# Six turns of K and q moved in the slot plan of an attention and SwiGLU kernel, two clearings moved forward

## The chip, the cores and the metric

The kernel runs on one core of a Trainium2 chip. The metric is the time of one execution on the device, in microseconds (us), of that core. The kernel before takes 325.97 us (median of three runs, 325.8 to 326.26).

## The reference, cut to what matters

```python
# attention: q, k, v are (4, 8, 768, 64), proj is (64, 6)
q_bits = (einsum('bhsd,dk->bhsk', q, proj) > 0)
k_bits = (einsum('bhsd,dk->bhsk', k, proj) > 0)
mask   = q_bucket[:, :, :, None] == k_bucket[:, :, None, :]   # all 6 bits equal
scores = where(mask, (q @ k.T) / 8, -1e9)
attn   = exp(scores - max); attn = attn / (sum(attn) + 1e-9)
x      = (attn @ v) as (3072 tokens, 512)
# feed-forward: w_gate and w_val (512, 1536), w_out (1536, 512)
xn  = x / sqrt(mean(x * x) + 1e-6) * rms_g
out = (silu(xn @ w_gate) * (xn @ w_val)) @ w_out
```

The mask is made inside the score product. Each of K and q gets twelve more rows behind its 64 rows of data: flags of 16 or -32 that tell on which side of each of the six planes a token lies. A pair of tokens with a differing bit gets a large negative score, so no compare and no select is needed.

## The kernel before, in words

**Windows and slots.** There are four batches of eight heads with 768 tokens. Half a batch's queries (384) are a window `w`, so there are eight windows. For a window and a head the scores are made in three slots: in each, TensorE multiplies two blocks of 128 keys with the 384 queries (L379, two matmuls into one of two `s_ps` buffers of PSUM), and ScalarE takes the exponential of both (`probs`, L389). There are 192 slots. The list `TURNS` orders the first 96 by pairs of heads: window 0 with pair 0, window 1 with pair 0, window 0 with pairs 1, 2 and 3, window 1 with pairs 1, 2 and 3, then the same for windows 2 and 3. Six slots go to each entry; slots 18 to 23 are window 0 with pair 2, and 24 to 29 window 0 with pair 3.

**The plan.** The order on every engine is written by hand. `at(s, f, ...)` puts a step into slot `s`, with a rank. The loop at the end runs through the slots: in slot `s` it first issues the scores of slot `s + 1`, then the steps of rank below 3, then the exponential of slot `s + 1`, then the other steps by rank and in the order in which they were planned. Every engine runs its instructions in that order and waits for what each one needs. SyncE issues most DMAs, one after the other.

**Turns.** The product needs K and q with the 64 features on the partitions. For batch 0 and for pairs 0 and 1 of batch 1 (`BY_PE`) TensorE turns them: `turn_pe` (L181) makes three 128 x 128 transposes of one head's K, or of its q, in fp32, into a bank `t_ps`. VectorE copies the bank to `kT` or `qT` (L189, in `keep`); `keep_pair(b, hp, i)` does that for i = 0 to 3: K and q of the pair's first head, then K and q of its second. One slot later `casts` has GpSimd write them as fp16 into the pair's buffer `QK` (L197). For all later pairs VectorE turns (`turn_dve`, L205), eight steps in a row.

**Flags.** `hash_heads` (L221) multiplies K and q of both heads of a pair with the planes on TensorE (`d_ps`), VectorE makes flags of the signs (`signs`, L228), and they are moved into rows 64 to 75 of `QK`: half of them by VectorE copies in the slots that follow (L300), half by four DMAs of SyncE (L298). For pair 2 of batch 0 that is planned at slot 12, for pair 3 at slot 17, for pair 0 of batch 1 at slot 33.

**Banks.** `t_ps`, `d_ps`, the sums of V (`m_ps`, L360) and all banks of the feed-forward share three banks of PSUM in turn. The sums of attention times V (`o_ps`, L401, nine matmuls a step, in two of three slots) have one place of their own.

**Buffers of K and q.** Six `QK` buffers are used in turn: batch 0 takes 0 to 3, batch 1 takes 4, 5, 0 and 1, batch 2 takes 2 to 5, batch 3 takes 0 to 3. A score product over 76 rows reads the data and the flags; one over 128 rows reads 52 rows more, which must be zero. `clear_rows(i)` has GpSimd fill rows 64 to 127 of buffer `i` with zeros (L139). Buffers 4 and 5 are cleared at the start, 2 and 3 at slots 76 and 78, 0 and 1 at slots 97 and 98. `score_rows` tells which products run over 128 rows.

**Feed-forward.** From slot 42 on, the feed-forward of window `w` (norm, gate L495, value L505, projection L519) is planned into the slots of later windows, 24 slots a window; behind slot 191 only feed-forward is left.

Of the kernel before, what the change touches and what calls it, by code (L numbers as in the profile page):

```python
# [22 lines left out]
KROWS = D + 12  # L23
# [25 lines left out]
def kernel(  # L49
# [89 lines left out]
        nc.gpsimd.memset(qkbuf[i][D:128].rearrange("p h n -> p (h n)").bitcast(FP32), 0.0)  # L139

    def score_rows(b, hp):
        return slice(0, 128 if (b, hp) in ((1, 0), (1, 1)) or b > 1 else KROWS)

    def t_tile(b, hp, which):
        T0[b, hp, which] = tpool.tile(
# [7 lines left out]
    def k_cols(b, h, jt):  # L153
        o = (jt // 3) * S + (jt % 3) * 128 if (b, h // 2) in BY_PE else S + jt * 128
        return QK[b, h // 2][score_rows(b, h // 2), h % 2, o : o + 128]

    def q_cols(w, h):
        b, half = divmod(w, 2)
        t = QK[b, h // 2][score_rows(b, h // 2), h % 2]
        if (b, h // 2) in BY_PE:  # L160
            return t[:, half * S + HALF : (half + 1) * S]
        if b == 1:
            return t[:, 0:S].rearrange("p (c e t) -> p e c t", e=2, t=128)[:, half]
        return t[:, half * HALF : (half + 1) * HALF]
# [472 lines left out]
    def at(s, f, *a, rank=3):  # L637
        plan[s].append((rank, len(plan[s]), lambda: f(*a)))
# [19 lines left out]
        at(1 + h, cast_half, 0, h, "q", 1)  # L658
        at(h, (bits0, bits1)[h], (nc.vector,), 3)

    for hp, turns, sv in ((1, (1, 2, 3, 5), 8), (2, (7, 8, 9, 10), 17), (3, (12, 13, 14, 15), 22)):
        for i, s in enumerate(turns):
            at(s, keep_pair, 0, hp, i)
            at(s + 1, casts, 0, hp, i)
            if i % 2:
                at(s + 2, cast_half, 0, 2 * hp + i // 2, "q", 0, nc.scalar)
        at(sv, v_prep, 0, hp)
# [17 lines left out]


    for hp, loads, turns, sh, evens, sv in (
        (0, (9, 11, 13), (20, 21, 24, 27), 33, (41, 42), (27, 44)),
        (1, (13, 14, 36), (29, 31, 33, 35), 40, (45, 47), (49, 51)),
    ):  # L690
        for which, sl in zip("kqv", loads):
            at(sl, load_rows, nc.sync, 1, hp, which)
        for i, sl in enumerate(turns):
            at(sl, keep_pair, 1, hp, i)
            at(sl + 1, casts, 1, hp, i)
        at(sh, hash_pair, 1, hp)
        for hh, sl in enumerate(evens):
            at(sl, cast_half, 1, 2 * hp + hh, "q", 0)
        at(sv[0], v_prep, 1, hp)
        at(sv[1], v_sum, 1, hp)  # L700
# [32 lines left out]
    for hp, s in enumerate((48, 62, 64, 78)):  # L733
        at(s, v_mean, 1, hp, 2)

    for i, s in ((2, 76), (3, 78), (0, 97), (1, 98)):
        at(s, clear_rows, i, rank=6)

    gts, sqs = {}, {}
# [20 lines left out]
    for w in range(8):  # L760
# [16 lines left out]
        for c in range(3):  # L777
            if w:
                s = {1: (58, 58, 59), 2: (84, 84, 85), 7: (202, 202, 202)}.get(
                    w, (s0 - 11, s0 - 10, s0 - 9))[c]  # L780
# [71 lines left out]
```

## Time and profile before

| | |
|---|---|
| median of three runs | 325.97 us (325.8 to 326.26) |
| profiled execution, whole | 325.82 us |
| its span in the trace | 324.0 us |
| TensorE, matmuls (PE) busy | 318.1 us, 98% |
| VectorE (DVE) busy | 232.6 us, 72% |
| ScalarE (ACT) busy | 208.2 us, 64% |
| GpSimd (POOL) busy | 167.5 us, 52% |
| chain that ended last | PE 94%, DMA 2%, ACT 2% |

The profile comes from one execution on the chip. Times in the trace count from the start of the span; the execution's own time is 1.82 us more than the span. PE is TensorE's matmuls, PEld its weight loads, SPq the queue on which SyncE issues DMAs. In the timeline a row gives the start in us, the time from the start of the row's first instruction to the end of its last, the engine, line, operation, what is written and read, the shape, how many instructions are merged, and in square brackets the idle time ahead of it with what ended it. Matmuls overlap, so the distance from one row's start to the next one's is what a row costs TensorE, not its length.

### The profile page before, as it was taken

Reading aid. Unit: us, or ns where it says so; the run is one execution under the profiler, and the core shown is the slowest. Engines: PE = TensorE matmul, PEld = TensorE weight load, DVE = VectorE, ACT = ScalarE, POOL = GpSimd, SP = SyncE. Lnnn points to the kernel's source line nnn. Section 1 sums busy time; section 2 is a strip of 40 time slices with the busy share of each in tenths; the row PEclk is TensorE's granted clock in tenths of the full one; section 3 lists DMA queues with packets and bytes.
Section 4 is the critical chain, followed back from the end, with each engine's and each line's share of the span. In section 5 each row is a group of like instructions: output and inputs, shape, how many; then the busy total and the mean of one; then the engine's idle time right before and its main releaser. Section 6 shows DMA issues by size and latency. Waiting matters only on the chain.

```text
span 324.0 us, 7728 instructions
## 1 busy us (share of the span) xinstructions
PE 318.1 (98%) x2927; PEld 196.3 (61%) x2927; DVE 232.6 (72%) x517; ACT 208.2 (64%) x324; POOL 167.5 (52%) x238
## 2 busy tenths in 40 slices
PE   8998999999999999999999999999999999999996
PEld 7676766655566556655556656566566656655654
DVE  4798897799598985889387865968167833793860
ACT  3788987775576666657576766657677766433321
POOL 8887977279768696686844275733220321230000
PEclk9999999999999999999999999999999999999999
DMA  7998989986488326962370753002200021004002
GB/s 234 353 210 247 166 127 185 163 182 106 134 143 162 71 59 132 199 127 56 121 130 17 139 95 113 3 18 46 72 32 2 17 67 65 2 1 131 1 2 97
DMA packets 91028, 34.25 MB, mean 106 GB/s; under 512 B 75992, under 2 KB 87920, under 8 KB 90992
## 3 DMA queue, kind: packets, MB, share of 16 engines
q1 hardware_dynamic: 86912, 28.85, 37.9%
q0 software_dynamic: 3712, 4.72, 9.4%
q8 instruction: 23, 0.38, 0.5%
q10 hardware_dynamic: 368, 0.20, 0.2%
q14 instruction: 13, 0.11, 0.1%
HBM read 28.58 MB, written 6.29 MB: 108 GB/s over the span
## 4 chain that ended last, share of the span: by engine, by line
PE 94%; DMA 2%; ACT 2%; DVE 0%; issue 0%; DVEq 0%; ACTq 0%
PE v_ps L505 19%; PE s_ps L379 19%; PE y_ps L519 18%; PE g_ps L495 16%; PE o_ps L401 10%; PE d_ps L221 4%; PE s_ps L495 4%; PE t_ps L181 2%; DMA QK<-bits 2%; ACT psb L389 1%; PE z_ps L372 1%; DMA out_dram<-ysb 1%; PE m_ps L360 1%; PE x_ps L480 0%; DVE bits L228 0%
## 5 line engine op out<-in xcount | busy, mean ns | idle before, releaser
L389 ACT ACTIVATE psb<-s_ps 128x768 f16<-128x768 f32 x192 | 150.7, 809 | 29.0 <-PE s_ps L379 27.2
L379 PE MATMUL s_ps<-QK 128*128 128x384 f16 (+1 forms) x384 | 93.6, 326 | 1.2 <-DMA QK<-bits 0.4
L505 PE MATMUL v_ps<-xnT,wv 128*128 128x384 f16 x384 | 78.1, 326 | 0.0
L519 PE MATMUL y_ps<-wo,ht 128*128 128x512 f16 x276 | 68.9, 379 | 0.0
L428 POOL TENSOR_TENSOR x<-otmp,rcp 128x384 f32<-128x384 f32 x30 | 25.8, 859 | 82.9 <-DVE rcp L421 82.7
L506 DVE SCALAR_TENSOR_TENSOR t<-t,g_ps 128x384 f32<-128x384 f32 x78 | 42.8, 549 | 34.1 <-ACT t L497 34.0
L401 PEld LDWEIGHTS <-psb 128*128 128x128 f16 x1152 | 51.8, 98 | 21.8 <-issue 3.8
L497 ACT ACTIVATE t<-g_ps 128x384 f32<-128x384 f32 x78 | 38.3, 491 | 40.8 <-PE g_ps L495 37.2
L495 PE MATMUL g_ps<-xnT,wg 128*128 128x384 f16 x312 | 63.4, 326 | 0.0
L507 DVE SCALAR_TENSOR_TENSOR ht<-t,v_ps 128x384 f16<-128x384 f32 x96 | 53.2, 554 | 10.5 <-PE v_ps L505 1.2
L401 PE MATMUL o_ps<-vl,psb 128*128 128x65 f16 x1152 | 56.0, 193 | 0.0
L505 PEld LDWEIGHTS <-wv 128*128 128x128 f16 x384 | 36.4, 98 | 23.1 <-issue 0.3
L495 PEld LDWEIGHTS <-wg 128*128 128x128 f16 x384 | 36.1, 98 | 23.0
L519 PEld LDWEIGHTS <-ht 128*128 128x128 f16 x276 | 26.6, 98 | 27.6 <-issue 1.9
L379 PEld LDWEIGHTS <-QK 128*128 128x128 f16 (+1 forms) x384 | 31.1, 97 | 16.7 <-issue 3.1
L526 ACT COPY ysb<-y_ps 128x512 f32<-128x512 f32 x23 | 13.5, 586 | 22.3 <-PE y_ps L519 21.7
L416 DVE TENSOR_TENSOR otmp<-o_ps,cvb 128x390 f32<-128x390 f32 x32 | 17.8, 557 | 12.7 <-PE o_ps L401 12.7
L440 POOL TENSOR_TENSOR sq<-x 128x384 f32<-128x384 f32 x30 | 25.5, 849 | 2.4
L213 POOL CAST QK<-kT 64x768 f16<-64x768 f32 x20 | 17.1, 853 | 8.4 <-DVE kT L205 6.7
L213 POOL CAST QK<-qT 64x768 f16<-64x768 f32 x20 | 16.4, 821 | 9.6 <-DVE qT L205 8.9
L205 DVE STREAM_TRANSPOSE kT<-kL 128x192 f32<-128x192 f32 x40 | 19.5, 521 | 0.1
L205 DVE STREAM_TRANSPOSE qT<-qL 128x192 f32<-128x192 f32 x40 | 19.1, 518 | 0.0
(82 smaller groups left out, 297.1 us busy)
## 6 DMA issues: line engine op xcount, KB each, us to landing
vL<-in_v_dram SPq DMA_DIRECT2D x16, 384.0 KB
out_dram<-ysb SPq DMA_DIRECT2D x23, 256.0 KB
kL<-in_k_dram SPq DMA_DIRECT2D x40, 96.0 KB
qL<-in_q_dram SPq DMA_DIRECT2D x40, 96.0 KB
kL<-in_k_dram SPq DMA_DIRECT2D x5, 384.0 KB
qL<-in_q_dram SPq DMA_DIRECT2D x5, 384.0 KB
wg<-in_moe_w_gate_dram POOLq DMA_DIRECT2D x2, 768.0 KB, 8.6
wv<-in_moe_w_val_dram POOLq DMA_DIRECT2D x2, 768.0 KB, 9.7
```

What stands on the lines that cost most here:

```text
L205: nc.vector.transpose(dst.rearrange("p (c t r) -> p r c t", c=6, r=4)[:, r : r + 1], src.rearrange("p (r c) d -> p r c d", r=4)[:, r : r + 1],
L213: nc.gpsimd.tensor_copy(QK[b, hp][0:64, hh, o : o + S], T0[b, hp, which][64 * hh : 64 * hh + 64, :])
L379: nc.tensor.matmul(ps[:, j, 0:HALF], k_cols(w // 2, h, 2 * p + j), q_cols(w, h), start=True, stop=True,)
L389: nc.scalar.activation(psb[w, h][:, p], sps.pop(g)[:, :, 0:HALF], AF.Exp, scale=ESCALE,)
L401: nc.tensor.matmul(o[:, c, hh, 0:65], psb[w, h][:, jt // 2, jt % 2, 128 * c : 128 * c + 128], vls[b % 2][:, h, v_chunk(b, h, jt), 0:65], s ...
L428: eng.tensor_mul(xd.rearrange("p c (h d) -> p c h d", h=2), tmp[:, :, :, 0:64], r.to_broadcast([128, 3, 2, 64]),)
L495: nc.tensor.matmul(g, wg[:, kt, fs], xnT[w][:, kt], start=(kt == 0), stop=(kt == 3))
L497: nc.scalar.activation(t, g, AF.Tanh, scale=0.5)
L505: nc.tensor.matmul(vv, wv[:, kt, fs], xnT[w][:, kt], start=(kt == 0), stop=(kt == 3))
L506: nc.vector.scalar_tensor_tensor(out=t, in0=t, scalar=1.0, in1=g, op0=ALU.add, op1=ALU.mult)
L507: nc.vector.scalar_tensor_tensor(out=ht[w][:, ft], in0=t, scalar=0.5, in1=vv, op0=ALU.mult, op1=ALU.mult)
L519: nc.tensor.matmul(y, ht[w][:, ft, c * 128 : (c + 1) * 128], wo[:, ft, :], start=(ft == 0), stop=(ft == NF - 1),)
```

## The change

Two things are moved, and one follows from the second.

First, in three pairs of heads the four turns are planned as two double steps: K and q of a head stand in one slot, one right behind the other. Pair 3 of batch 0 goes from slots 12, 13, 14, 15 to 13, 13, 15, 15; pair 0 of batch 1 from 20, 21, 24, 27 to 21, 21, 25, 25; pair 1 of batch 1 from 29, 31, 33, 35 to 30, 30, 34, 34. The casts stay one slot behind their turn. Pairs 1 and 2 of batch 0 keep their slots.

Second, buffers 0 and 1 are cleared at slots 49 and 50, before pairs 2 and 3 of batch 1 are written into them, no longer at 97 and 98. So the products of these two pairs can run over 128 rows too, and do: all scores behind batch 0 now take 128 rows.

```diff
     def score_rows(b, hp):
-        return slice(0, 128 if (b, hp) in ((1, 0), (1, 1)) or b > 1 else KROWS)
+        return slice(0, 128 if b else KROWS)
...
-    for hp, turns, sv in ((1, (1, 2, 3, 5), 8), (2, (7, 8, 9, 10), 17), (3, (12, 13, 14, 15), 22)):
+    for hp, turns, sv in ((1, (1, 2, 3, 5), 8), (2, (7, 8, 9, 10), 17), (3, (13, 13, 15, 15), 22)):
         for i, s in enumerate(turns):
             at(s, keep_pair, 0, hp, i)
             at(s + 1, casts, 0, hp, i)
...
     for hp, loads, turns, sh, evens, sv in (
-        (0, (9, 11, 13), (20, 21, 24, 27), 33, (41, 42), (27, 44)),
-        (1, (13, 14, 36), (29, 31, 33, 35), 40, (45, 47), (49, 51)),
+        (0, (9, 11, 13), (21, 21, 25, 25), 33, (41, 42), (27, 44)),
+        (1, (13, 14, 36), (30, 30, 34, 34), 40, (45, 47), (49, 51)),
     ):
...
-    for i, s in ((2, 76), (3, 78), (0, 97), (1, 98)):
+    for i, s in ((0, 49), (1, 50), (2, 76), (3, 78)):
         at(s, clear_rows, i, rank=6)
```

## The prediction

> **What bounds the kernel now.** I read the page first, then the timelines of TensorE and ScalarE up to 48 us, then VectorE, GpSimd and the DMA queue around the moved steps.
>
> ```profile
> span 324.0 us, 7728 instructions
> PE 318.1 (98%) x2927; PEld 196.3 (61%) x2927; DVE 232.6 (72%) x517; ACT 208.2 (64%) x324; POOL 167.5 (52%) x238
> ...
> PE   8998999999999999999999999999999999999996
> ...
> L389 ACT ACTIVATE psb<-s_ps 128x768 f16<-128x768 f32 x192 | 150.7, 809 | 29.0 <-PE s_ps L379 27.2
> ```
>
> TensorE is busy throughout; its only thin slices are among the first four and the last (a slice is 8.1 us). The number of matmuls does not change, so the time changes only by what TensorE waits. From slot 42 on feed-forward matmuls fill its slots. Before that a slot holds little more than scores and attention times V, and there ScalarE sets the pace:
>
> ```profile
> 33.71 0.48 PE L379 MATMUL s_ps<-QK 76*128 76x384 f16 x2
> 34.03 0.44 PE L401 MATMUL o_ps<-vl,psb 128*128 128x65 f16 x9
> 34.41 0.48 PE L379 MATMUL s_ps<-QK 76*128 76x384 f16 x2
> 34.73 0.43 PE L401 MATMUL o_ps<-vl,psb 128*128 128x65 f16 x9
> 35.12 0.48 PE L379 MATMUL s_ps<-QK 76*128 76x384 f16 x2
> ...
> 36.56 0.48 PE L379 MATMUL s_ps<-QK 76*128 76x384 f16 x2
> 36.88 0.49 PE L181 MATMUL t_ps<-ident,kL 128*128 128x128 f32 x3
> 37.21 0.44 PE L401 MATMUL o_ps<-vl,psb 128*128 128x65 f16 x9
> 37.48 0.49 PE L379 MATMUL s_ps<-QK 76*128 76x384 f16 x2
> 37.81 0.51 PE L360 MATMUL m_ps<-vl,ones 128*128 128x130 f16 x6
> 38.16 0.44 PE L401 MATMUL o_ps<-vl,psb 128*128 128x65 f16 x9
> 38.43 0.49 PE L379 MATMUL s_ps<-QK 76*128 76x384 f16 x2
> 38.76 0.49 PE L181 MATMUL t_ps<-ident,qL 128*128 128x128 f32 x3
> 39.09 0.44 PE L401 MATMUL o_ps<-vl,psb 128*128 128x65 f16 x9
> 39.36 0.94 PE L379 MATMUL s_ps<-QK 76*128 76x384 f16 x4
> 40.23 0.51 PE L221 MATMUL d_ps<-kT,pk 128*32 128x384 f32 x1
> ...
> 41.02 0.55 PE L181 MATMUL t_ps<-ident,kL 128*128 128x128 f32 x3
> 41.40 0.49 PE L379 MATMUL s_ps<-QK 76*128 76x384 f16 x2
> ```
>
> ```profile
> 28.83 3.83 ACT L389 ACTIVATE psb<-s_ps 128x768 f16<-128x768 f32 x5 [0.84 <-PE s_ps L379]
> ...
> 39.95 1.51 ACT L389 ACTIVATE psb<-s_ps 128x768 f16<-128x768 f32 x2 [0.18 <-PE s_ps L379]
> 41.93 2.34 ACT L389 ACTIVATE psb<-s_ps 128x768 f16<-128x768 f32 x3 [0.47 <-PE s_ps L379]
> ```
>
> Counted from the first score, the pair at 33.71 is slot 26, those at 36.56, 37.48 and 38.43 are slots 30, 31 and 32, the four matmuls at 39.36 are slots 33 and 34, and 41.40 is slot 35; the exponential at 28.83 is slot 19's. By the distances from start to start a score pair costs TensorE 0.33, a turn 0.33, nine matmuls of attention times V 0.27, the sum of V 0.35, and the eight of a hash, from the end of slot 34's pair (39.36 + 0.94 - 0.48 + 0.32 = 40.14) to 41.02, 0.88. In slots 26 and 27 TensorE has 0.60 of work, but the pairs lie 0.70 and 0.71 apart: with two `s_ps` buffers it must wait for the exponential two slots back. Two exponentials in a row take 1.51 and one takes 0.81, so their step is 0.70 to 0.71.
>
> ```profile
> 48.59 0.65 PE g_ps L495 x4
> ...
> 86.14 0.65 PE g_ps L495 x4
> ```
>
> The chain in order of time has window 0's first gate, in slot 42, at 48.59 and window 1's, in slot 66, at 86.14. So there is a simple ledger up to slot 42. **A slot whose TensorE work is over 0.71 makes ScalarE idle for the excess, and a slot with less gives nothing back**, for TensorE cannot run further ahead. Only a small lag is free: an exponential starts 0.53 behind its pair (41.40 to 41.93), while the buffer allows the pair 2 x 0.71 - 0.81 - 0.05 = 0.56 ahead, 0.05 being the semaphore's way, an estimate from these rows. That leaves 0.03.
>
> **The pairs of batch 1 (slots 20 to 35), the main term.** Turns that stood alone beside a light slot cost nothing: slots 24 and 27 held score pair and turn only, 0.33 + 0.33 = 0.66. These free places are given up.
>
> Before, behind slot 23: slot 29 (pair, turn, o_ps) 0.93, excess 0.22 - 0.03 = 0.19; slot 30 (pair, m_ps, o_ps) 0.95, excess 0.24; slot 31 like slot 29, 0.22; slot 33 (hash and turn) by the trace's own row 0.47 idle plus the 0.10 by which exponentials otherwise overlap, 0.57; slot 35 (pair, turn, o_ps) 0.22, less 0.11 that TensorE wins in the light slot 34, 0.11. Sum 1.33.
>
> After: slot 25 (pair, two turns, o_ps) 0.33 + 0.66 + 0.27 = 1.26, excess 0.55 - 0.03 = 0.52; slot 30 (pair, m_ps, two turns, o_ps) 1.61, excess 0.90 - 0.03 = 0.87; slot 33 (pair, hash) 1.21, excess 0.50 - 0.03 = 0.47; slot 34 (pair, two turns, o_ps) 0.55. Sum 2.41, so 1.08 more. Slots 20 to 22 hold the same work before and after, but slot 20 is now light and wins nothing, and slot 21 has both turns: before 0.19 + 0.17, after 0.23 + 0.24, 0.11 more. **Together +1.2 us** at slot 42. Two small waits of TensorE for the norm of window 0 (slots 38 to 40) are covered then; I count -0.1 for them, an estimate. VectorE's two copies a pair (0.56 each, below) fall together too, but each ends before its bank is asked for again, three banks later. GpSimd's casts move with their turns by a slot; their `QK` is read from slot 48 on.
>
> **Pair 3 of batch 0 (slots 12 to 15).** Here VectorE has no pause:
>
> ```profile
> 21.00 0.56 DVE L189 COPY qT<-t_ps 128x384 f32<-128x384 f32 x1
> 21.59 0.25 DVE L272 COPY QK<-bits 12x384 f16<-12x384 f16 x1
> 21.87 0.56 DVE L189 COPY kT<-t_ps 128x384 f32<-128x384 f32 x1
> 22.48 0.68 DVE L228 TENSOR_SCALAR bits<-d_ps,thr,scl 128x384 f16<-128x384 f32 x1
> ```
>
> ```profile
> 23.19 3.34 SPq L298 DMA_DIRECT2D QK<-bits  x4
> ...
> 28.28 3.06 SPq L298 DMA_DIRECT2D QK<-bits  x4
> ```
>
> ```profile
> 28.47 0.65 PE L379 MATMUL s_ps<-QK 76*128 76x384 f16 x3 [0.39 <-DMA QK<-bits]
> ```
>
> The order of instructions shows that the K turn of slot 12 goes behind pair 2's hash. The hash needs the q copy that ends at 21.56, so it ends when it did, and the signs still start at 22.48; the K copy at 21.87 no longer fills that gap. VectorE runs half a microsecond late from slot 15 on, by the step of two copies, and so pair 3's hash, its signs and the four DMAs at 28.28 (SyncE's loads of K and q behind them, too) come 0.5 later. TensorE is late by the same half microsecond at slot 18, but there it waited 0.39 for pair 2's flags, which left at 23.19 and leave then again: absorbed, 0.1 either way. Pair 3's flags are needed in slot 25, one step before 33.71 and so 4.7 behind 28.28; pair 2's took from 23.19 to 28.47, 5.3. If they are as slow, slot 25 waits up to 0.5; it may also land as before, for SyncE issues loads of V, K and q just ahead of them that have to pass first. I take 0, by the loads. ScalarE's own casts of this pair stay at slots 15 and 17, two behind the q turns, which keep their slots; SyncE's order does not change at all, and the rows of K are released a slot later to a load that stands eight DMAs further back.
>
> **128 rows and the clearings.**
>
> ```profile
> L379 PE MATMUL s_ps<-QK 128*128 128x384 f16 x240 | 58.6, 326 | 0.0
> ...
> L379 PE MATMUL s_ps<-QK 76*128 76x384 f16 x144 | 35.0, 325 | 1.2 <-DMA QK<-bits 0.4 <-ACT psb L389 0.3 <-ACT qT L189 0.2
> ```
>
> ```profile
> L139 POOL MEMSET QK<- 64x1536 f32 x6 | 8.2, 1374 | 0.3
> ```
>
> ```profile
> 57.04 0.82 POOL L345 CAST vl<-vL 128x768 f16<-128x768 f32 x1
> 63.67 0.83 POOL L428 TENSOR_TENSOR x<-otmp,rcp 128x384 f32<-128x384 f32 x1 [5.81 <-DVE rcp L421]
> ...
> 69.87 0.20 POOL L453 TENSOR_SCALAR ms<-ss 128x3 f32<-128x3 f32 x1 [0.79 <-DVE ss L451]
> ```
>
> A matmul takes 326 ns over 128 rows and 325 over 76; 48 change, 0 to -0.1 us for the steps between them. The clearing of slot 49 (1.37) fits into GpSimd's 5.81 of idle time from 57.86. That of slot 50 comes behind the two operations from 63.67 on, at about 65.4, and pushes the sums of V, the K casts and the norm (69.87) by 1.37 less 0.79 of idle: 0.6. The norm feeds window 1's first gate, 16 us later at 86.14. So 0; with that cover gone, 0.6. Slots 97 and 98 lose two clearings beside which nobody waited.
>
> [...] No row here has a clearing that blocks VectorE; its chance is part of the late waits' below.
>
> **The sum.** +1.2 - 0.1 + 0 - 0.05 + 0 = +1.05, say +1.0. The profiled execution took 325.82 (span 324.0 and 1.82 around it) and would take 326.8. The median of the runs, 325.97, lies 0.15 above it, so I predict **327.0 us**. This case's own range is 326.5 (a coupling 0.5 looser) to 327.6 (0.5 for late flags).
>
> **Rivals.** *ScalarE's pace is not passed on* (or the pairs do no more than change the order): if TensorE could run one slot further ahead, light slots 24 and 27 would pay for 25 and 30, and the main term would be about 0: 325.8 to 326.1. For it: the ledger counts ScalarE's idle time, and the end is TensorE's. Against it: the steps of 0.70 at 33.71 to 35.12 with 0.60 of work. Chance 0.17.
>
> *Late waits* pile onto the forecast: flags of pair 3 and the norm of window 1, 0.5 + 0.6 on top: 328.1. Chance 0.08.
>
> *Not slower: pair 2's flags land sooner.* ScalarE idled 0.84 before 28.83, and TensorE's wait for them ended just then; their DMA takes 5.3 us among the loads. If VectorE, without the K copy, reaches the signs before 22.48 and the DMA slips ahead of a load, up to 0.84 comes back: 327.0 - 0.84 = 326.2; with a main term half as large, 325.6, and with none, 325.1. It decides at whether the signs start before 22.48. Against it: the q copy that ends at 21.56. Chance 0.13.
>
> **How the numbers follow.** Forecast 0.62, the three rivals 0.17, 0.08 and 0.13. About 0.2% (0.65 us) is what a measurement of this kernel can tell from no change. Slower by over 0.2% (over 326.62): 0.57 of the forecast's 0.62 and the 0.08, so 0.65. Faster by over 0.2% (under 325.32): the lower ends of the first and the last rival, 0.05 each, 0.10. Within: 0.25. The range reaches down to 325.9, into the first rival, and up to 327.7.
>
> **What would show it.** Right: pair 2's signs start within 0.1 of 22.48; ScalarE's exponentials of slots 27, 32, 35 and 36 each have about half a microsecond of idle ahead of them (0.9 for 32); the first gate comes near 49.6, and behind it every stage keeps its distance. Wrong: the first gate at 48.6 or before, or a wait of TensorE behind 60 us that names GpSimd or a DMA of flags.

## The result and the profile after

| | before | after |
|---|---|---|
| median | 326.1 us (325.8 to 326.4, 6 runs) | 327.05 us (326.82 to 327.68, 6 runs) |
| profiled execution, whole | 325.82 us | 327.11 us |
| its span | 324.0 us | 325.3 us |

The changed kernel takes 1.0033 times as long as the kernel before (95% interval 1.002 to 1.0046), 0.95 us by the medians. The forecast was 327.0 us.

The page of the changed kernel shows the same work, spread over more time. These are its first lines, TensorE's row of slices and the group of the exponentials:

```profile
span 325.3 us, 7723 instructions
PE 318.2 (98%) x2927; PEld 195.9 (60%) x2927; DVE 232.9 (72%) x517; ACT 207.7 (64%) x324; POOL 166.8 (51%) x238
...
PE   8998999999999999999999999999999999999996
...
L389 ACT ACTIVATE psb<-s_ps 128x768 f16<-128x768 f32 x192 | 150.4, 809 | 31.0 <-PE s_ps L379 29.5
```

TensorE's busy time (318.1 and 318.2) and the exponential (809 ns) are unchanged; ScalarE's idle time ahead of exponentials grows from 29.0 to 31.0. The page does not say where. The chain of waits of the changed kernel, in order of time, does so roughly, by its first gates of windows 0 and 1:

```profile
50.00 0.65 PE g_ps L495 x4
...
87.53 0.65 PE g_ps L495 x4
```

Before, these stood at 48.59 and 86.14. So 1.41 is lost by the first gate and 1.39 by the second: all of the loss lies ahead of slot 42, and nothing between the two gates adds to it.

ScalarE's timeline of the changed kernel, by start, length, instructions in the row and idle time ahead of it, gives the slots:

```profile
29.10 3.88 ACT L389 ACTIVATE psb<-s_ps 128x768 f16<-128x768 f32 x5 [1.33 <-PE s_ps L379]
33.18 2.21 ACT L389 ACTIVATE psb<-s_ps 128x768 f16<-128x768 f32 x3 [0.20 <-PE s_ps L379]
35.88 3.66 ACT L389 ACTIVATE psb<-s_ps 128x768 f16<-128x768 f32 x5 [0.49 <-PE s_ps L379]
40.28 2.22 ACT L389 ACTIVATE psb<-s_ps 128x768 f16<-128x768 f32 x3 [0.74 <-PE s_ps L379]
42.87 0.81 ACT L389 ACTIVATE psb<-s_ps 128x768 f16<-128x768 f32 x1 [0.38 <-PE s_ps L379]
44.19 4.42 ACT L389 ACTIVATE psb<-s_ps 128x768 f16<-128x768 f32 x6 [0.51 <-PE s_ps L379]
```

The row at 29.10 holds the exponentials of slots 19 to 23; counting on, the next rows begin with slots 24, 27, 32, 35 and 36. Exponentials otherwise overlap by 0.10, so a bracket of 0.49 is a loss of 0.59. The losses ahead of slots 27, 32, 35 and 36 are 0.59, 0.84, 0.48 and 0.61. Behind slot 36 five steps run without a break.

TensorE's timeline of the changed kernel at the pair's heaviest place, slot 30:

```profile
38.15 0.49 PE L379 MATMUL s_ps<-QK 76*128 76x384 f16 x2
38.47 0.51 PE L360 MATMUL m_ps<-vl,ones 128*128 128x130 f16 x6
38.82 0.49 PE L181 MATMUL t_ps<-ident,kL 128*128 128x128 f32 x3
39.15 0.49 PE L181 MATMUL t_ps<-ident,qL 128*128 128x128 f32 x3
39.48 0.44 PE L401 MATMUL o_ps<-vl,psb 128*128 128x65 f16 x9
39.75 0.49 PE L379 MATMUL s_ps<-QK 76*128 76x384 f16 x2
```

From score pair to score pair are 1.60 us, all of it work and none of it a wait. ScalarE's step is 0.71, so it stands idle for the rest.

**A caution on the size.** When slot 19 starts differs from execution to execution. In the profiles before and after, TensorE's last wait ahead of it is for the flags of pair 2, which by the chain of waits take 5.15 us from issue to landing before and 5.61 after. Slot 19's exponential starts at 28.83 before and at 29.10 after. The edit does not set this: in the seven kernels of this document with the plan of the kernel before up to slot 19 it starts at 28.59 to 29.37, in the four with pair 3 moved at 28.47 to 29.27. TensorE's timelines have the first gate, in the kernel before and in the changed kernel, at

```profile
48.43 0.81 PE L495 MATMUL g_ps<-xnT,wg 128*128 128x384 f16 x4
```

```profile
49.84 0.81 PE L495 MATMUL g_ps<-xnT,wg 128*128 128x384 f16 x4
```

so from that exponential to the gate are 19.60 and 20.74. So the change itself accounts for **1.14** of the 1.41, and the other 0.27 is how the flags landed in these two executions. The medians, 0.95 apart, agree better with the 1.14 than with the whole difference of the profiles. In each experiment I use the median for the verdict. To say why, I use the stretch from slot 19's exponential to the first gate, 19.60 before, where slot 19 comes no sooner than before; a sooner start is lost again in slot 22, as the kernel with only the rows and the clearings shows below.

### The profile page after: what moved, and what is told of

It reads as the page before. It is cut to its first block, busy times and chain, and to the rows that moved or that the text cites. A ratio compares the mean times of both kernels' runs of the same rounds, so it can differ in the third digit from the quotient of the medians.

```text
span 325.3 us, 7723 instructions
## 1 busy us (share of the span) xinstructions
PE 318.2 (98%) x2927; PEld 195.9 (60%) x2927; DVE 232.9 (72%) x517; ACT 207.7 (64%) x324; POOL 166.8 (51%) x238
## 4 chain that ended last, share of the span: by engine, by line
PE 94%; DMA 2%; ACT 2%; DVE 0%; issue 0%; DVEq 0%; ACTq 0%
PE v_ps L505 19%; PE s_ps L379 19%; PE y_ps L519 18%; PE g_ps L495 16%; PE o_ps L401 10%; PE d_ps L221 4%; PE s_ps L495 4%; PE t_ps L181 2%; DMA QK<-bits 2%; ACT psb L389 2%; PE z_ps L372 1%; DMA out_dram<-ysb 1%; PE m_ps L360 1%; PE x_ps L480 0%; DVE bits L228 0%
```

## The experiments

The change moves nine turns, two of pair 3, three of pair 0 and four of pair 1, so that all the turns of these pairs form six double steps. The kernel before was run beside each experiment; its median there is 326.11 or 326.14. My theory: a slot whose TensorE work is over ScalarE's step of 0.71 costs the excess, and the light slots given up cost nothing by themselves. Rivals: the pairing itself costs; pair 3 delays the flags; the rows or the clearings cost.

### Only pair 0 of batch 1

```diff
-        (0, (9, 11, 13), (20, 21, 24, 27), 33, (41, 42), (27, 44)),
+        (0, (9, 11, 13), (21, 21, 25, 25), 33, (41, 42), (27, 44)),
```

> Only pair 0 of batch 1 goes to slots 21, 21, 25, 25; the rest as before. Ledger: slot 25 costs 0.52 and slots 20 to 22 cost 0.11 more, slots 24 and 27 were free and give nothing back: +0.6 us, seen as 0.5 to 0.6 of idle ahead of the exponential of slot 27, and slots 31 to 37 as before. Rival, the pairing itself costs (two turns in a row through banks and copies): then slots 21 and 25 cost alike, and the sum is over 0.9. Rival, nothing is passed on: 0.

326.64 us, ratio 1.0014 (1.0001 to 1.0026), 0.5 more than before. Its ScalarE timeline has the loss of slot 27, and behind it the rows look like those of the kernel before:

```profile
32.93 2.21 ACT L389 ACTIVATE psb<-s_ps 128x768 f16<-128x768 f32 x3 [0.20 <-PE s_ps L379]
35.63 4.78 ACT L389 ACTIVATE psb<-s_ps 128x768 f16<-128x768 f32 x6 [0.49 <-PE s_ps L379]
```

The 0.49 at 35.63 is the bracket that the changed kernel has at 35.88. The ledger holds here.

### Only pair 1 of batch 1

```diff
-        (1, (13, 14, 36), (29, 31, 33, 35), 40, (45, 47), (49, 51)),
+        (1, (13, 14, 36), (30, 30, 34, 34), 40, (45, 47), (49, 51)),
```

> Only pair 1 of batch 1 goes to slots 30, 30, 34, 34; the rest as before. Ledger: 0.87 + 0.47 + 0.55 for slots 30, 33 and 34 in place of 1.33 for slots 29, 30, 31, 33 and 35: +0.56 us. Rival, nothing is passed on: 0. Rival, the turns gain by standing together in this stretch, which held five costly slots: below 0.

326.87 us, ratio 1.0027 (1.0014 to 1.0039), 0.73 more, somewhat above the forecast. ScalarE's loss ahead of slot 32 is a bracket of 1.03, not 0.74, in its timeline:

```profile
39.63 2.21 ACT L389 ACTIVATE psb<-s_ps 128x768 f16<-128x768 f32 x3 [1.03 <-PE s_ps L379]
```

TensorE's timeline of this kernel has the turns of slot 30, and VectorE's the copies:

```profile
37.88 0.50 PE L181 MATMUL t_ps<-ident,kL 128*128 128x128 f32 x3
38.44 0.55 PE L181 MATMUL t_ps<-ident,qL 128*128 128x128 f32 x3
38.83 0.44 PE L401 MATMUL o_ps<-vl,psb 128*128 128x65 f16 x9
```

```profile
37.84 0.55 DVE L189 COPY qT<-t_ps 128x384 f32<-128x384 f32 x1
38.31 0.28 DVE L363 TENSOR_SCALAR cvb<-m_ps 128x130 f32<-128x130 f32 x1
```

The q turn follows the K turn after 0.56 instead of 0.33. It takes the third bank behind that of slot 27's q, and VectorE copies that q out only from 37.84 to 38.39; the turn starts 0.05 later. So three banks do not always cover two turns in one slot, as the prediction had counted on. In the whole change the q of pair 0 is turned two slots sooner, and this wait is not there: the two turns at 38.82 and 39.15 above follow each other without one.

### Only pair 3 of batch 0

```diff
-    for hp, turns, sv in ((1, (1, 2, 3, 5), 8), (2, (7, 8, 9, 10), 17), (3, (12, 13, 14, 15), 22)):
+    for hp, turns, sv in ((1, (1, 2, 3, 5), 8), (2, (7, 8, 9, 10), 17), (3, (13, 13, 15, 15), 22)):
```

> Only pair 3 of batch 0 goes to slots 13, 13, 15, 15; batch 1, rows and clearings as before. The ledger says that nothing before slot 18 reaches the end, because TensorE waits there for the flags of pair 2 anyway: 0 to +0.1 us, with the flags' DMA issued and landing as before (from issue to TensorE's score 5.3 us). The rival, late flags: that the exponential of slot 19 came 0.27 us later in the changed kernel although the DMA was issued 0.19 earlier is caused by this move; then slot 19's exponential is 0.3 to 0.5 later here too, with 1.3 us of idle ahead of it for 0.84, and the time +0.3 to +0.5.

326.92 us, ratio 1.0023 (1.0014 to 1.0033): 0.78 more, where I had expected 0 to 0.1. Not the flags: slot 19's exponential starts at 28.63, sooner than before, and slot 25 waits for nothing. TensorE's timeline of this kernel shows the place, slot 22:

```profile
31.40 0.51 PE L360 MATMUL m_ps<-vl,ones 128*128 128x130 f16 x6
32.77 0.43 PE L401 MATMUL o_ps<-vl,psb 128*128 128x65 f16 x9 [0.86 <-DVE otmp L416]
```

The sums `o_ps` have one place in PSUM, so those of slot 22 wait until VectorE has read those of slot 20 (`otmp`). VectorE's timeline of this kernel says why it was late, and GpSimd's why that was:

```profile
30.71 0.55 DVE L444 TENSOR_REDUCE ssp<-sq 128x3 f32<-128x384 f32 x1 [0.82 <-POOL sq L440]
...
31.56 0.56 DVE L189 COPY kT<-t_ps 128x384 f32<-128x384 f32 x1
32.15 0.56 DVE L416 TENSOR_TENSOR otmp<-o_ps,cvb 128x390 f32<-128x390 f32 x1
```

```profile
26.59 1.05 POOL L197 CAST QK<-kT 64x384 f16<-64x384 f32 x2 [0.92 <-DVE kT L189]
```

The casts of pair 3 start late on GpSimd, behind VectorE's late K copy; the sum of squares `sq` stands behind them in GpSimd's order; `ssp` waits for it and starts at 30.71 and not at 29.94, and `otmp` comes behind `ssp` and behind the K copy of slot 20. In the kernel before, the same two rows on VectorE and TensorE stand just far enough apart:

```profile
31.38 0.56 DVE L416 TENSOR_TENSOR otmp<-o_ps,cvb 128x390 f32<-128x390 f32 x1
```

```profile
31.99 0.43 PE L401 MATMUL o_ps<-vl,psb 128*128 128x65 f16 x9
```

The read ends at 31.94 and the sums start 0.05 later, where TensorE's previous work would have let them start at 31.60 + 0.35 = 31.95. There was no slack left, and the 0.77 of delay reaches TensorE (31.99 to 32.77).

### Only the rows and the clearings

```diff
-        return slice(0, 128 if (b, hp) in ((1, 0), (1, 1)) or b > 1 else KROWS)
+        return slice(0, 128 if b else KROWS)
...
-    for i, s in ((2, 76), (3, 78), (0, 97), (1, 98)):
+    for i, s in ((0, 49), (1, 50), (2, 76), (3, 78)):
```

> The turns as before; only the two clearings at slots 49 and 50 and 128 rows for pairs 2 and 3 of batch 1. 48 matmuls of the same length and clearings in idle time of GpSimd: 0 to -0.1 us. Rival, the clearing at slot 50 holds up the norm of window 1 or blocks VectorE: +0.3 to +0.6, with TensorE waiting between 57 and 90 us.

326.11 us, ratio 1.0003 (0.9993 to 1.0013): no effect that can be measured, as forecast. The plan up to slot 49 is that of the kernel before, and yet slot 19's exponential starts 0.22 sooner, at 28.61, and the first gate 0.08 later, at 48.51. TensorE's timeline of this kernel has the place where the head start is lost, slot 22:

```profile
32.08 0.43 PE L401 MATMUL o_ps<-vl,psb 128*128 128x65 f16 x9 [0.19 <-DVE otmp L416]
```

There TensorE waits for `otmp`, as with pair 3 alone but for less. So a stretch of 19.90, as here, is no cost when slot 19 came early.

The four parts alone cost 0.78, 0.5, 0.73 and about 0, which is 2.0; together they cost 0.95. So some of these waits must be ones that another part of the change removes. The next two kernels test that for pair 3.

### Pair 3 as changed, and the K turn of slot 20 one slot later

```diff
-    for hp, turns, sv in (... (3, (12, 13, 14, 15), 22)):
+    for hp, turns, sv in (... (3, (13, 13, 15, 15), 22)):
...
-        (0, (9, 11, 13), (20, 21, 24, 27), 33, (41, 42), (27, 44)),
+        (0, (9, 11, 13), (21, 21, 24, 27), 33, (41, 42), (27, 44)),
```

> Pair 3 of batch 0 in slots 13, 13, 15, 15 as in the run with this pair alone, and the K turn of slot 20 one slot later (21, 21, 24, 27). In that run attention times V of slot 22 waited 0.86 us for VectorE's addition of slot 20, which reads the only place of o_ps and stood behind the K copy of slot 20. If that queue on VectorE is the cause, the copy goes behind the addition now, the wait is gone, the exponential of slot 24 has 0.3 of idle ahead of it and not 1.27, and the time is the kernel before's +0.1 (0 to +0.25). If pair 3 costs in another way: +0.8 stays.

326.42 us, ratio 1.0004 (0.9995 to 1.0013). The 0.78 shrinks to 0.3 by the median and to 0.1 by the ratio, and TensorE's timeline of this kernel has the sums of slot 22 without a wait, though GpSimd's casts and `ssp` on VectorE are late here too:

```profile
32.14 0.51 PE L360 MATMUL m_ps<-vl,ones 128*128 128x130 f16 x6
32.49 0.43 PE L401 MATMUL o_ps<-vl,psb 128*128 128x65 f16 x9
```

The K copy now stands behind `otmp` on VectorE, as pair 0's move has it in the whole change. From slot 19's exponential (29.27) to the gate (48.90) are 19.63, where the kernel before has 19.60.

### The whole change without pair 3

```diff
-    for hp, turns, sv in (... (3, (13, 13, 15, 15), 22)):
+    for hp, turns, sv in (... (3, (12, 13, 14, 15), 22)):
```

> The changed kernel with pair 3 of batch 0 back in slots 12 to 15. By the queue on VectorE, pair 3 costs nothing there, since the K copy of slot 20 is out of the way: as the changed kernel, 327.0 (326.8 to 327.1). If the costs of the parts simply add: 0.8 less, 326.3.

Here the diff is against the changed kernel. 327.26 us, ratio 1.003 (1.0019 to 1.004), somewhat above the expected range and not to be told from the changed kernel's 1.0033. Taking pair 3's move out brings nothing back: within the whole change it costs nothing that can be measured, where each interval is some 0.4 us to either side. The stretch to the first gate, 20.72 (29.37 to 50.09), is the changed kernel's too. So the sum of the parts can be mended: without pair 3's 0.78, and without the 0.29 by which the wait for a bank lengthened a bracket in pair 1's part (1.03 and not 0.74), 0.5 and 0.73 leave 0.94, about the 0.95 measured.

### Pairs, but in light slots

```diff
-        (0, (9, 11, 13), (20, 21, 24, 27), 33, (41, 42), (27, 44)),
-        (1, (13, 14, 36), (29, 31, 33, 35), 40, (45, 47), (49, 51)),
+        (0, (9, 11, 13), (21, 21, 24, 24), 33, (41, 42), (27, 44)),
+        (1, (13, 14, 36), (27, 27, 32, 32), 40, (45, 47), (49, 51)),
```

> K and q of a head still turned one right behind the other in both pairs of batch 1, but in slots without attention times V: 21, 21, 24, 24 and 27, 27, 32, 32 (pair 3 of batch 0, rows and clearings as in the kernel before). If the place costs and not the pairing, each double slot has 0.98 of work and 0.24 of excess in place of 0.5 to 0.9: slots 21, 22, 24, 27, 30, 32, 33 sum to 1.9 against the 1.8 measured before: +0.1 us (0 to +0.3). If the pairing itself costs: about as the two pairs cost alone, +0.5 and +0.7, so over +0.8.

325.8 us, ratio 0.9992 (0.9984 to 1.0001). The same two pairs, doubled in the same way, in slots that hold no attention times V, cost nothing and may even save 0.3, a little less than the expected 0 to +0.3. Of ScalarE's breaks between slots 20 and 41 of this kernel the largest left is that of the hash, ahead of slot 35:

```profile
36.86 4.72 ACT L389 ACTIVATE psb<-s_ps 128x768 f16<-128x768 f32 x6 [0.15 <-PE s_ps L379]
41.99 5.12 ACT L389 ACTIVATE psb<-s_ps 128x768 f16<-128x768 f32 x7 [0.41 <-PE s_ps L379]
```

A pair of turns with a score pair is 0.99, an excess of 0.28, where beside attention times V it was 0.55, and beside the sum of V as well 0.90. **The place costs, not the pairing.**

### The whole change, with the two pairs in those slots

```diff
-        (0, (9, 11, 13), (21, 21, 25, 25), 33, (41, 42), (27, 44)),
-        (1, (13, 14, 36), (30, 30, 34, 34), 40, (45, 47), (49, 51)),
+        (0, (9, 11, 13), (21, 21, 24, 24), 33, (41, 42), (27, 44)),
+        (1, (13, 14, 36), (27, 27, 32, 32), 40, (45, 47), (49, 51)),
```

> The whole changed kernel (pair 3 at 13, 13, 15, 15, clearings at 49 and 50, 128 rows), with the two pairs of batch 1 in light slots: 21, 21, 24, 24 and 27, 27, 32, 32 in place of 21, 21, 25, 25 and 30, 30, 34, 34. The ledger: the loss of the change lies in slots 25, 30 and 34 alone, so 1.0 to 1.2 comes back, and the time is that of the kernel with light pairs and nothing else, 325.8, at most 0.2 more for pair 3: 325.8 to 326.1. The rival: turns of K and q one behind the other cost by themselves, or pair 3 costs the 0.8 that it cost alone; then 326.5 to 327.

Again the diff is against the changed kernel. 326.28 us, ratio 1.0004 (0.9996 to 1.0013): most of the 0.95 is back, but the time lies above the expected 325.8 to 326.1. Where the rest comes from stays open. The profiled execution cannot tell, for it is the fastest of the eleven, at 325.84, with its first gate at 48.49, where the kernel before has 48.43. Its TensorE waits again in slot 22:

```profile
31.34 0.51 PE L360 MATMUL m_ps<-vl,ones 128*128 128x130 f16 x6
31.98 0.43 PE L401 MATMUL o_ps<-vl,psb 128*128 128x65 f16 x9
```

The sums could have started at 31.69 and start at 31.98, behind `otmp`, which ends at 31.93 on VectorE. But `otmp` starts where it does in the kernel before (31.37 and 31.38), and the kernel with only the rows and the clearings, whose pair 3 is not moved, has this wait too. In both executions slot 19's exponential came early (28.47 and 28.61), and TensorE reached slot 22 sooner than VectorE was ready; in the profile of the whole change it came at 29.10 and there is no such wait. So the wait is the price of an early start and not of pair 3's move. This rests on single executions.

### Turns alone in light slots

```diff
-        (0, (9, 11, 13), (20, 21, 24, 27), 33, (41, 42), (27, 44)),
-        (1, (13, 14, 36), (29, 31, 33, 35), 40, (45, 47), (49, 51)),
+        (0, (9, 11, 13), (17, 18, 19, 21), 33, (41, 42), (27, 44)),
+        (1, (13, 14, 36), (24, 27, 32, 36), 40, (45, 47), (49, 51)),
```

> The eight turns of batch 1 as singles in slots that are light: 17, 18, 19, 21 and 24, 27, 32, 36 (the rest as in the kernel before). Ledger: what is left is slot 22 (0.2 to 0.3), slot 30 (0.24) and the hash of slot 33 (0.5), about 1.0 against 1.8: -0.8 us, or -0.5 if the norm of window 0 is what ends last then. Rival, TensorE's early waits are set by VectorE and the flags: 0.

326.13 us, ratio 1.0000 (0.9991 to 1.0009). Nothing of the expected gain: the rival's course. What the turns of slots 29, 31, 33 and 35 cost is gone, but two waits for VectorE came in their place on TensorE:

```profile
33.15 0.43 PE L401 MATMUL o_ps<-vl,psb 128*128 128x65 f16 x9 [0.39 <-DVE otmp L416]
...
47.26 0.51 PE L221 MATMUL d_ps<-kT,pk 128*32 128x384 f32 x1 [0.19 <-DVE xnT L481]
```

The copies of the turns moved into slots 17 to 21 hold up `otmp`, and the norm of window 0 comes no sooner than VectorE makes it. The stretch from slot 19's exponential to the first gate is 19.84 (29.42 to 49.26), against 19.60 before. The 29.42 is not the flags: TensorE does not wait for them here, and the turns of slots 17 and 18 stand ahead of it, so some of the cost may lie before the stretch.

### Half a hash in each of two light slots

The pairs stand in the light slots, and the hash of pair 0, the last heavy step, is split by columns over slots 33 and 36; its signs go with the second half.

```diff
-        at(sh, hash_pair, 1, hp)
+        if hp == 0:
+            at(33, hash_part, 1, 0, 0)
+            at(36, hash_part, 1, 0, 1)
+            at(36, hash_pair, 1, 0)
+        else:
+            at(sh, hash_pair, 1, hp)
```

> The pairs in light slots as before (pair 0 of batch 1 at 21, 21, 24, 24, pair 1 at 27, 27, 32, 32), and the hash of pair 0, which makes slot 33 heavy (0.33 + 0.88 against 0.71), is split by columns: the first 192 columns in slot 33, the other 192 and the signs in slot 36, which holds a score pair only. Same work in sum. The ledger: each half is about 0.34 + 0.10, so slots 33 and 36 have 0.77 each, an excess of 0.06 twice in place of 0.50. The idle of 0.5 ahead of the exponential of slot 35 goes, the first gate comes 0.4 earlier, and the time is about 0.4 below the 325.8 of the kernel with light pairs: 325.4. The rival: the gain does not reach the gate, because the norm of window 0 (VectorE, slots 37 to 40) is paced by VectorE's queue and the signs come later into it; then the idle goes ahead of slot 35 and comes back ahead of slots 38 to 42, and the time stays at 325.7 to 326.0.

326.37 us, ratio 1.0005 (0.9994 to 1.0016): the rival's course, and beyond its range. ScalarE's break ahead of slot 35 is gone (slots 29 to 39 now stand in one row), and it is back later:

```profile
37.27 8.60 ACT L389 ACTIVATE psb<-s_ps 128x768 f16<-128x768 f32 x11 [0.15 <-PE s_ps L379]
46.12 1.51 ACT L389 ACTIVATE psb<-s_ps 128x768 f16<-128x768 f32 x2 [0.25 <-PE s_ps L379]
48.79 0.81 ACT L389 ACTIVATE psb<-s_ps 128x768 f16<-128x768 f32 x1 [1.15 <-PE s_ps L379]
```

The last bracket was 0.88 with the whole hash. VectorE's timeline of this kernel shows what waits:

```profile
43.96 0.68 DVE L228 TENSOR_SCALAR bits<-d_ps,thr,scl 128x384 f16<-128x384 f32 x1 [0.71 <-PE d_ps L657]
44.55 1.93 DVE L468 TENSOR_SCALAR xn<-x,rstd 128x512 f16<-128x512 f32 x3
```

The signs wait 0.71 for the second half of the hash, and the norm's `xn` stands behind them, at 44.55; with the whole hash in slot 33 it starts at 43.33. The executions differ by 0.41 at slot 19, so 0.81 of that delay is the edit's. The stretch to the first gate is 19.83 (29.30 to 49.13), against 19.45 (28.89 to 48.34) with the whole hash. From slot 37 on the norm on VectorE, not ScalarE's pace, leads to the gate.

## Why the prediction was right

**The ledger of heavy slots** was right, in size and in place. It gave +1.2 at slot 42 with -0.1 for the norm; measured from slot 19's exponential to the gate it is +1.14. Its four marks were 0.52, 0.87, 0.47 and 0.55 ahead of slots 27, 32, 35 and 36; measured are 0.59, 0.84, 0.48 and 0.61. Of the 0.1 for the norm little shows: from its first transposes on TensorE (L480) to the gate are 3.79 before and 3.76 after. The part kernels of pairs 0 and 1 show each half of it, that of pair 1 with the wait for a bank on top, and the kernel with pairs in light slots shows that the rule, and not the pairing, carries the loss. The rival that ScalarE's pace is not passed on would have left the gate at 48.6; it is at 50.00 in the chain of waits.

**Pair 2's signs** start at 22.29 in VectorE's timeline of the changed kernel, behind a gap where the K copy had been:

```profile
22.29 0.68 DVE L228 TENSOR_SCALAR bits<-d_ps,thr,scl 128x384 f16<-128x384 f32 x1 [0.65 <-PE d_ps L221]
```

That is 0.19 before 22.48, outside the 0.1 that I had named, but TensorE runs 0.18 sooner already ahead of the first moved turn (slot 13's scores start at 20.44 and not 20.62), so the edit did not do it; with pair 3 alone the signs start at 22.50. The rival of sooner flags is refuted: they still end a wait of TensorE, in the changed kernel at 28.74:

```profile
28.74 0.65 PE L379 MATMUL s_ps<-QK 76*128 76x384 f16 x3 [0.53 <-DMA QK<-bits]
```

**Pair 3** was right in its sum, 0, and incomplete in its reason. Its four DMAs leave half a microsecond later, as predicted (28.28 before), in the queue of the changed kernel:

```profile
28.73 3.06 SPq L298 DMA_DIRECT2D QK<-bits  x4
```

Slot 25 does not wait for them. But the prediction followed VectorE's delay only into the flags. It missed that the delay goes on, through GpSimd's casts and squares, to `otmp` of slot 20, on which TensorE's single place for `o_ps` hangs: alone that costs 0.78. In the whole change it cost nothing only because pair 0's K copy moved out of the way, which the prediction did not see either. A right sum hid a wrong step.

**Banks.** "Each ends before its bank is asked for again" holds in the whole change and failed in pair 1's part alone (0.56 for 0.33).

**Rows and clearings** were right: 0.0 measured. The clearing of slot 50 stands where it was expected on GpSimd, and delays the sums of V behind it:

```profile
66.92 1.37 POOL L139 MEMSET QK<- 64x1536 f32 x1
68.38 1.00 POOL L351 TENSOR_TENSOR vadd<-vL 128x384 f32<-128x384 f32 x1
```

The second gate keeps its distance (1.41 and 1.39 above), so the norm's cover held; TensorE's waits in the changed kernel show none behind 57 us; and the rival of late waits is refuted.

**The range.** The median of 327.05 lies 0.05 from the forecast. Part of that closeness is luck: the six executions of the changed kernel alone lie 0.86 apart (326.82 to 327.68), and the prediction had neither pair 3's 0.78 nor the move that took it away again.

## What to carry to other kernels

Where one engine paces a stretch (here ScalarE, with 0.71 a slot) and the buffer ahead of it is two deep, add up the other engine's work slot by slot: here slots above the pace cost their excess (0.59 ahead of slot 27, 0.84 ahead of slot 32), and the light slots paid nothing back (1.14 was left at the first gate), so a step belongs where its slot has room for it and not beside its twin. A part that costs alone (0.78 for pair 3) may cost nothing in the whole when a one-place buffer stands at its edge; follow a delay through every queue it enters, not only to the consumer that the edit has in mind. And before a saving is counted, look at what comes next: here the freed time ahead of slot 35 was lost again at the norm (326.37 with the hash in two halves, 325.8 with it whole).

## What the runs showed of the hardware

A VectorE copy of 12 x 384 fp16 values from SBUF to SBUF takes 0.25 us alone (at 25.47 in the changed kernel, with GpSimd idle). Started just behind a GpSimd instruction of 0.82 us it took 0.83 in the kernel before and 0.94 in the changed one, and then ended about 0.1 behind that instruction. In VectorE's and GpSimd's timelines of the kernel with pair 3 alone:

```profile
28.96 0.93 DVE L300 COPY QK<-bits 12x384 f16<-12x384 f16 x1
```

```profile
28.95 0.82 POOL L428 TENSOR_TENSOR x<-otmp,rcp 128x384 f32<-128x384 f32 x1
```

Started just ahead of one it kept its 0.25, as in the two timelines of the changed kernel:

```profile
32.17 0.25 DVE L300 COPY QK<-bits 12x384 f16<-12x384 f16 x1
```

```profile
32.22 0.89 POOL L428 TENSOR_TENSOR x<-otmp,rcp 128x384 f32<-128x384 f32 x1 [1.01 <-DVE rcp L421]
```

In these rows 0.93 is GpSimd's 0.82 and some 0.1 more, and the copy that started first was not held up. Why that is so no run here shows, and some copies beside GpSimd's casts kept their 0.25 too (the one at 24.39 in the changed kernel). The clearing at 66.92 does not hold up VectorE in this way: beside it VectorE turns K and works on gate banks, in instructions of 0.53 to 0.56 us, as long as in the kernel before without it (0.53 to 0.55).

The flags of pair 2, four DMAs among loads, took 5.15 us from issue to landing in the kernel before and 5.61 in the changed kernel, by their chains of waits, both at a granted clock of 1.0. Slot 19's exponential, behind them, starts up to 0.8 us apart in kernels with the same plan up to there (28.59 to 29.37). That is nearly as large as the whole effect of the change, and why the parts had to be read by stretches behind it.
